# Batch 0 of a two-block kernel: loads in another order, identity products in waits, a new hand-written order, and stores by quarters

## The chip, the core and the metric

The kernel runs on one core of a Trainium2 chip. What is measured is the device time of one execution in microseconds; the profile adds the span of the core and the TensorE clock that the throttle granted. Before the change the time is 767.9 us (median of three runs, 767.73 to 767.93).

## The reference

```
# attention block: x (B,H,S,D) = (8,8,512,64), state (8,8,32,64)
scores  = scale * x @ state.T        # per batch and head, 512 x 32
xread   = softmax(scores,  -1) @ state
scores2 = scale * state @ x.T        # 32 x 512
sread   = softmax(scores2, -1) @ x
y = concat([xread, sread], axis=2)   # (B,H,544,64)
# bridge: (B,H,544,64) -> rows (B*544, 512)
# feed-forward block, w_in 512 x 2048, w_out 2048 x 512, both float64 inputs
h = rows @ w_in
g = where(h > 0, h, exp(min(h, 0)) - 1)      # elu
out = g @ w_out
```

## The kernel before

For each batch the 512 token rows go through attention and the feed-forward block. The attention of the tokens isn't multiplied out: `make_m` forms M = state · w_in, and `ffn1` multiplies the turned softmax `aT` straight by M (8 matmul records of 128x512 for two of its 16 blocks `fo`). `exp_part` on ScalarE and `max_part` on VectorE make the elu, `ffn2_row` multiplies by `w_out` into four PSUM banks, `o_ps` = banks 0 to 3. Batches 1 to 7 use two levels of a Strassen scheme for the second product; after batch 7, `states()` runs the 256 state rows of all batches at once, with one such level (`Strassen(1)`), and stores them.

The weights arrive as float64. Each of 32 pieces (512 KB of HBM) is made float32 by three ScalarE instructions (`convert_1`) and four VectorE instructions (`convert_2`), all within batch 0. Batch 0 is therefore unlike the others: TensorE, VectorE and ScalarE all have much to do, and their order is written out by hand.

That order is the string `plan` in `first_batch`. Each token is a step, put on its engine in this order, and every engine keeps it (`InOrder`). The names that matter here:

- `kT`, `kTc`: turn the states on TensorE, copy them out of PSUM on VectorE into the tile `kT`
- `x:b.i`, `xc:b.i`: turn half of x of batch b on TensorE, copy it out on ScalarE; `sc:b`: scores on TensorE into banks 6 and 7
- `mx`, `sd`, `tr`, `tm`, `su`, `tt` (batch.group, VectorE), `ps`, `pm` (GpSimd), `ae`, `te` (ScalarE): the two softmaxes; `tt` writes `aT`
- `sT`, `sTc`, `sr`, `src`: the state's own read (TensorE, ScalarE, TensorE, ScalarE)
- `w:k.1`, `w:k.2`: `convert_1` and `convert_2` of weight piece k; after `w:k.2` the next load is issued (`fetch`)
- `M:0.c.h`, `Mc:0.c.h`: a half of M and its copy; `F:fo` is `ffn1`, `R:fo` is `exp_part`, `E:fo` is `max_part`, `O:fo` is `ffn2_row`

`load_states` loads the states of all eight batches with eight transfers, four on the SP queue and four on the ACT queue; `load_x` loads one batch of x with four. The first code lines that run are

```
raw_states = load_states()
load_x(0, [sync, scalar])
for k in range(NRAW - 1):
    fetch()
```

The raw pieces, the raw states and turned x share one pool of `NRAW + 4` = 11 buffers (tag `w`). At the end of batch 0 the four banks `o_ps` are copied out, bank 0 first, bank 3 last; banks 1 and 3 on VectorE. `ffn1` of batch 1 writes banks 4, 5, 3, 4, ... in turn, so its third block needs bank 3 back. From batch 1 on VectorE, ScalarE and GpSimd are ordered by the scheduler of the language, which also draws the weight sums of batch 1 (tiles `t_w`, `t`, `w_out`) in between the last steps of batch 0 on VectorE.

`states()` ends with eight stores of one batch each, 64 KB, all on the SP queue and all after the last step of the second product.

Of the kernel before, what the change touches and what calls it, by code (L numbers as in the profile page):

```python
# [10 lines left out]
FP32 = mybir.dt.float32  # L11
# [14 lines left out]
def kernel(  # L26
# [15 lines left out]
    B, H, S, D = x.shape  # L42
    NS = state.shape[2]
    DM, DF = moe_w_in.shape
    P = 128
    R = S // P
    NP = H // 2
    G = 2
    FO = DF // P
    FC = DF // 512  # L50
    SB = S + NS
    NB = S // 32
    NRAW = 7
# [6 lines left out]
    out_b = out.rearrange("(b s) c -> b s c", b=B)  # L60
# [4 lines left out]
    def pool(name, bufs, **kw):  # L65
        return ctx.enter_context(tc.tile_pool(name=name, bufs=bufs, **kw))

    cpool = pool("const", 1)
# [4 lines left out]
    work = pool("work", NRAW + 4)  # L73
# [6 lines left out]
    def bank(i):  # L80
        return psum[:, i]

    def pair(i):

        return psum[:, i : i + 2]
# [3 lines left out]
    class InOrder:  # L89
# [10 lines left out]
    tensor, sync, vector, scalar, gpsimd = (  # L100
        InOrder(e) for e in (nc.tensor, nc.sync, nc.vector, nc.scalar, nc.gpsimd)
    )
    matmul = tensor.matmul

    def transpose(out, in_):


        for t in range(2):
            rows = slice(t * 64, (t + 1) * 64)
            tensor.transpose(out[:, t], in_[rows], ident[rows, rows], tile_position=(t * 64, 0))  # L110
# [4 lines left out]
    ident = cpool.tile([P, P], FP32, name="ident")  # L115
# [6 lines left out]
    kT = cpool.tile([P, B, P], FP32, name="kT")  # L122
# [3 lines left out]
    x_t, st, m_t = {}, {}, {}  # L126
# [6 lines left out]
                out=x_t[b][:, r].rearrange("p (h d) -> p h d", d=D), in_=x_v[:, r]  # L133
            )

    def load_states():
        raw = work.tile([P, B, G, D], FP32, tag="w", name="s_sb")
        s_v = state.rearrange("b (m c) n d -> m c n b d", c=G)
        for m in range(NP):
            for c in range(G):  # L140
                (sync, scalar)[c].dma_start(out=raw[m * NS : (m + 1) * NS, :, c], in_=s_v[m, c])
        return raw

    def turn_states(raw):
        ps = st["k_ps"] = pair(6).rearrange("p t (b q) -> p t b q", q=64)
        for b in range(B):
            transpose(ps[:, :, b], raw[:, b].rearrange("p c d -> p (c d)"))

    def load_weights(src):
        _, n, k = src.shape  # L150
        raw = work.tile([P, n, k], moe_w_in.dtype, tag="w", name="raw")
        sync.dma_start(out=raw, in_=src)
        return raw
# [39 lines left out]
    def load_w_in(c, k):  # L193

        h, n = divmod(k, 2)
        rows = slice(2 * n, 2 * n + 2)
        cols = slice(c * 512 + h * 256, c * 512 + (h + 1) * 256)
        return w_in[:, 2 * c + h, rows], load_weights(w_in_v[:, rows, cols])

    def load_w_out(fo):  # L200
        raw = load_weights(w_out_v[:, fo : fo + 1])
        return w_out[:, fo : fo + 1], raw
# [168 lines left out]
    def max_part(fo, e, ps):  # L371
        vector.scalar_tensor_tensor(
            out=g_all[:, fo, : ps.shape[-1]], in0=e, scalar=-1.0, in1=ps,
            op0=ALU.add, op1=ALU.max,
        )
# [255 lines left out]
    def first_batch():  # L631

        plan = """
            kT kTc x:0.0 xc:0.0 w:0.1 x:0.1 xc:0.1 w:0.2 w:1.1 sc:0 mx:0.1 w:2.1 tr:0.1 tr:0.0
            tm:0.1 w:3.1 tm:0.0 ps:0.1 mx:0.0 w:1.2 ps:0.0 ae:0.1 ae:0.0 te:0.1 sT:0 sd:0.0 sd:0.1  # L640
            te:0.0 su:0.1 sTc:0 su:0.0 pm:0.1 w:4.1 M:0.0.0 w:3.2 pm:0.0 Mc:0.0.0 w:7.1 sr:0 tt:0.1
            tt:0.0 w:4.2 F:0 src:0 w:8.1 w:2.2 F:1 R:0 w:5.1 E:0 M:0.0.1 w:8.2 Mc:0.0.1 R:1 F:2
            w:5.2 w:9.1 O:0 E:1 w:10.1 w:9.2 R:2 F:3 w:10.2 w:6.1 M:0.1.0 O:1 E:2 Mc:0.1.0 w:6.2 R:3
            w:12.1 E:3 F:4 w:7.2 w:11.1 O:2 w:12.2 w:13.1 R:4 w:11.2 M:0.1.1 F:5 w:14.1 w:13.2 O:3
            R:5 Mc:0.1.1 E:4 w:16.1 E:5 w:14.2 F:6 w:17.1 M:0.2.0 w:16.2 F:7 R:6 w:15.1 E:6 O:4
            w:17.2 Mc:0.2.0 w:18.1 w:15.2 F:8 R:7 w:18.2 O:5 w:21.1 E:7 R:8 w:21.2 M:0.2.1 w:19.1
            O:6 E:8 w:23.1 w:19.2 Mc:0.2.1 F:9 w:23.2 w:24.1 O:7 w:25.1 w:24.2 w:20.1 w:25.2 F:10
            R:9 O:8 w:20.2 w:22.1 E:9 R:10 w:22.2 M:0.3.0 w:26.1 F:11 E:10 O:9 Mc:0.3.0 w:26.2 R:11
            w:27.1 E:11 M:0.3.1 w:29.1 w:27.2 F:12 O:10 R:12 w:29.2 Mc:0.3.1 w:30.1 E:12 F:13 w:31.1
            w:30.2 O:11 R:13 w:31.2 w:28.1 E:13 x:1.0 w:28.2 F:14 xc:1.0 x:1.1 R:14 F:15 xc:1.1 E:14  # L650
            sc:1 R:15 O:12 mx:1.0 mx:1.1 ae:1.0 tr:1.0 ae:1.1 tr:1.1 tm:1.0 sT:1 tm:1.1 ps:1.0 O:13
            sd:1.0 sTc:1 sd:1.1 E:15 ps:1.1 te:1.0 su:1.0 te:1.1 pm:1.0 su:1.1 sr:1 pm:1.1 tt:1.0
            O:14 src:1 tt:1.1 M:1.0 O:15 Mc:1.0
        """.split()
        make_identity(nc, ident)
        o_ps = [bank(c) for c in range(R)]
        order = [lambda k=k: load_w_in(0, k) for k in range(4)]
        for c in range(1, FC + 1):
            if c < FC:
                order += [lambda c=c, k=k: load_w_in(c, k) for k in range(4)]  # L660
            order += [lambda fo=fo: load_w_out(fo) for fo in range(4 * c - 4, 4 * c)]
        w, h, e = [], {}, {}

        def fetch():
            if len(w) < len(order):
                w.append(order[len(w)]())
            elif 1 not in x_t:
                load_x(1, [sync])

        raw_states = load_states()  # L670
        load_x(0, [sync, scalar])
        for k in range(NRAW - 1):
            fetch()
        groups = {
            "mx": column_max, "tr": turn_scores, "ae": column_exp, "tm": row_max,
            "ps": row_subtract, "te": row_exp, "su": row_sum, "pm": row_scale,
            "tt": turn_tokens, "sd": column_total,
        }
        whole = {
            "sc": scores, "sT": turn_state, "sTc": copy_state, "sr": state_read,  # L680
            "src": keep_read,
        }
        for step in plan:
            name, _, num = step.partition(":")
            num = [int(i) for i in num.split(".") if i]
            if name == "kT":
                turn_states(raw_states)
            elif name == "kTc":
                vector.tensor_copy(out=kT.rearrange("p b (t q) -> p t b q", t=2), in_=st["k_ps"])
                fetch()  # L690
            elif name in groups:
                groups[name](*num)
            elif name in whole:
                whole[name](*num)
            elif name == "w":
                (convert_1, convert_2)[num[1] - 1](*w[num[0]])
                if num[1] == 2:
                    fetch()
            elif name == "F":
                h[num[0]] = ffn1(0, num[0])  # L700
            elif name == "R":
                e[num[0]] = exp_part(h[num[0]])
            elif name == "E":
                max_part(num[0], e[num[0]], h[num[0]])
            elif name == "O":
                ffn2_row(o_ps, num[0])
            elif name == "x":
                turn_x(*num)
            elif name == "M":
                make_m(*num)  # L710
                if len(num) == 2:
                    make_m(1, 1, first=4)
            elif name == "xc":
                copy_x(*num)
            else:
                assert name == "Mc", step
                if len(num) == 3:
                    copy_half(*num)
                else:
                    for g in range(G):  # L720
                        copy_m(*num, g, scalar.copy)
        for g in range(G):
            copy_m(1, 1, g, scalar.copy)
        for i in range(2):
            o_sb = opool.tile([P, 2, DM], FP32, name="o_sb")
            for c in range(2):
                (scalar.copy, vector.tensor_copy)[c](out=o_sb[:, c], in_=o_ps[2 * i + c])
            store(0, i, o_sb)

# [26 lines left out]
    def states():  # L756
        for i in second:
            i.restore()
        for fo in range(FO):
            ffn1_state(fo)  # L760
        half = Strassen(1)
        half.sums()
        for f in half.steps():
            f()
        for b in range(B):
            c, i = divmod(b, P // NS)
            sync.dma_start(
                out=out_b[b, S:SB], in_=half.o_sb[c][i * NS : (i + 1) * NS].rearrange("p n c -> p (n c)")
            )

    first_batch()
    load_x(2, [sync])
# [35 lines left out]
```

## Time and profile before

Busy time of the engines in some stretches of the span (us from its start; records of matmuls overlap, so a TensorE busy for the whole stretch may have room in it):

| stretch | TensorE | VectorE | ScalarE | granted clock | DMA GB/s |
|---|---|---|---|---|---|
| 0 to 5 | 0.34 | 0.00 | 0.00 | 1.00 | 125 |
| 5 to 10 | 1.93 | 1.22 | 1.28 | 1.00 | 247 |
| 10 to 15 | 1.91 | 0.09 | 2.98 | 1.00 | 386 |
| 25 to 30 | 2.75 | 4.72 | 4.94 | 0.99 | 108 |
| 60 to 80 | 20.00 | 19.28 | 19.65 | 1.00 | 200 |
| 80 to 100 | 20.00 | 18.74 | 16.87 | 1.00 | 79 |
| whole span, 766.1 | 735.7 | 416.2 | 311.0 | 0.994 | 46 |

Up to some 40 us no engine is busy all the time; from there to about 110 us three are; after that TensorE alone is. A waiting instruction is put down to what released it last. "Chain" below is the chain of work that ended last, followed back from the last instruction. A name like `ps<-aT,m_sb` is what an instruction writes and reads, with the tile names of the code; `issue` means that the profile shows nothing waited for.

### The profile page before, as it was taken

To read this page: it belongs to the slowest core of one execution; us is meant where nothing else is said; L and a number is where in the kernel's file an instruction comes from. 1 tells how busy PE (TensorE), PEld (TensorE's weight loads), DVE (VectorE), ACT (ScalarE), POOL (GpSimd) and SP (SyncE) were. 2 spreads that over 40 slices of the span, in tenths; PEclk is the share of its full clock that TensorE was granted. 3 is DMA by queue.
4 is the path that set the end of the run, shared out by engine and by line. 5 is a ranking of instruction groups with operands and counts; after the bars stand their busy time and mean duration, and the time that the engine had idled before them with its cause. 6 is when DMAs were issued, how large, how long until landed. Compare 5 with 4: busy or idle time off the path is not lost.

```text
span 766.1 us, 10566 instructions
## 1 busy us (share of the span) xinstructions
PE 735.7 (96%) x4352; PEld 502.0 (66%) x4352; DVE 416.2 (54%) x737; ACT 311.0 (41%) x557; POOL 35.1 (5%) x38
## 2 busy tenths in 40 slices
PE   3599999999999999999999999999999999999996
PEld 1234444368955787478946895578747894689885
DVE  2999989638246533655354824663365535534230
ACT  4799874553036312641065303631264106400420
POOL 0200002002000200010000200020001000000000
PEclk9899999999999999999999999999999999999999
DMA  9555400400210021002000021002100000000001
GB/s 282 216 196 212 110 1 1 110 1 10 46 56 1 1 56 56 0 2 56 28 27 1 13 44 55 1 1 56 56 1 2 1 31 25 0 1 28 29 1 27
DMA packets 44849, 35.29 MB, mean 46 GB/s; under 512 B 36352, under 2 KB 36352, under 8 KB 44800
## 3 DMA queue, kind: packets, MB, share of 16 engines
q1 hardware_dynamic: 41632, 33.82, 14.6%
q10 hardware_dynamic: 3168, 0.79, 0.5%
q8 instruction: 34, 0.56, 0.3%
q14 instruction: 15, 0.12, 0.1%
HBM read 25.69 MB, written 8.91 MB: 45 GB/s over the span
## 4 chain that ended last, share of the span: by engine, by line
PE 92%; DVE 5%; DMA 1%; ACT 1%; issue 0%; ACTq 0%; DVEq 0%
PE ps L95 92%; DVE t_w L95 1%; DMA x_sb<-in_x_dram 1%; DVE w_in L95 1%; DVE total_t L95 1%; DVE w_out L95 0%; DMA s_sb<-in_state_dram 0%; ACT raw L95 0%; DVE top L95 0%; DVE aT L95 0%; DVE top_t L95 0%; ACT xT L95 0%; DVE t_sb L95 0%; ACT a_s L95 0%; ACT e_sb L95 0%; DVE o_sb L95 0%
## 5 line engine op out<-in xcount | busy, mean ns | idle before, releaser
L95 PE MATMUL ps<-w_out,g_all 128*128 128x256 f32 (+2 forms) x1088 | 252.2, 385 | 0.0
L95 PE MATMUL ps<-aT,m_sb 128*128 128x512 f32 x512 | 228.4, 600 | 6.2 <-DVE aT L95 3.3
L95 PEld LDWEIGHTS ps<-w_out,g_all 128*128 128x128 f32 x1088 | 188.8, 190 | 57.4 <-issue 35.9
L95 PEld LDWEIGHTS ps<-aT,m_sb 128*128 128x128 f32 x512 | 96.3, 192 | 128.6 <-issue 118.6
L95 DVE SCALAR_TENSOR_TENSOR g_all<-e_sb,ps 128x512 f32<-128x512 f32 (+1 forms) x144 | 94.2, 656 | 118.5 <-ACT e_sb L95 118.5
L95 ACT ACTIVATE e_sb<-ps 128x512 f32<-128x512 f32 (+1 forms) x144 | 82.5, 573 | 179.0 <-PE ps L95 161.3
L95 DVE TENSOR_TENSOR o_sb<-o_sb,ps 128x128 f32<-128x128 f32 (+2 forms) x122 | 43.8, 359 | 138.5 <-PE ps L95 96.9
L95 PE MATMUL ps<-t_w,s 128*128 128x256 f32 x480 | 107.2, 379 | 0.0
L95 PEld LDWEIGHTS ps<-t_w,s 128*128 128x128 f32 x480 | 90.7, 190 | 12.1
L95 ACT ACTIVATE e_sb<-e_sb 128x512 f32<-128x512 f32 (+1 forms) x144 | 87.3, 606 | 4.5
L95 ACT COPY o_sb<-ps 128x512 f32<-128x512 f32 (+1 forms) x34 | 19.1, 562 | 165.2 <-PE ps L95 115.9
L95 ACT ACTIVATE raw<-raw 128x512 f32<-128x512 uint32 x64 | 43.6, 682 | 1.0
L95 POOL TENSOR_TENSOR t_sb<-t_sb,top_t 128x512 f32<-128x512 f32 x16 | 17.6, 1108 | 536.0 <-DVE top_t L95 536.0
L95 PE MATMUL ps<-w_in,kT 64*32 64x512 f32 (+1 forms) x576 | 33.5, 553 | 0.0
L95 DVE TENSOR_TENSOR g_all<-g_all,s 128x512 f32<-128x512 f32 (+1 forms) x30 | 27.8, 926 | 9.6 <-PE ps L95 9.6
L95 PE MATMUL ps<-t_w,g_all 128*128 128x128 f32 (+1 forms) x240 | 32.0, 282 | 0.0
L95 DVE TENSOR_REDUCE top<-ps 128x1 f32<-128x512 f32 x16 | 11.0, 685 | 38.6 <-PE ps L95 38.6
L95 PEld LDWEIGHTS ps<-t_w,g_all 128*128 128x128 f32 x240 | 30.3, 192 | 0.8
L95 DVE TENSOR_TENSOR s<-s,g_all 128x512 f32<-128x512 f32 (+1 forms) x30 | 27.0, 934 | 3.4 <-PE ps L95 3.4
L95 DVE TENSOR_TENSOR g_all<-g_all 128x512 f32<-128x512 f32 (+1 forms) x30 | 28.1, 937 | 0.6
L95 DVE TENSOR_TENSOR s<-g_all 128x512 f32<-128x512 f32 (+1 forms) x30 | 27.5, 937 | 0.6
L95 PE MATMUL ps<-xT_state,w_in 128*128 128x256 f32 x128 | 27.8, 379 | 0.0
(67 smaller groups left out, 476.4 us busy)
## 6 DMA issues: line engine op xcount, KB each, us to landing
raw<-in_moe_w_in_dram SPq DMA_DIRECT2D x16, 512.0 KB, 5.8
raw<-in_moe_w_out_dram SPq DMA_DIRECT2D x16, 512.0 KB, 3.7
out_dram<-o_sb SPq DMA_DIRECT2D x16, 512.0 KB, 2.6
x_sb<-in_x_dram SPq DMA_DIRECT2D x30, 256.0 KB, 4.4
x_sb<-in_x_dram ACTq DMA_DIRECT2D x2, 256.0 KB, 5.8
out_dram<-o_sb SPq DMA_DIRECT2D x8, 64.0 KB, 1.7
s_sb<-in_state_dram ACTq DMA_DIRECT2D x4, 64.0 KB, 3.1
s_sb<-in_state_dram SPq DMA_DIRECT2D x4, 64.0 KB, 2.8
```

The source lines that it names most:

```text
L95: ins = getattr(self.engine, name)(*args, **kw)
```

## The change

It touches batch 0 and the last stores:

1. x of batch 0 is loaded first; of the states only batch 0's, 32 KB on each of two queues, into a tile of its own (`s_first`). The states of batches 1 to 7 are loaded by eight transfers on SP once 12 weight pieces have been asked for, and turned by the new steps `kU` and `kUc` in mid-batch. Seven weight pieces instead of six are asked for ahead.
2. `Z:n` issues n products of the identity with itself into bank 3, which nobody reads. They are to keep TensorE active while it waits.
3. The order of batch 0 is another.
4. Bank 3 is copied out first at the end of batch 0, then 2, 1, 0.
5. `states()` stores a quarter of its result (128 rows by 256 columns) as soon as it is done; the last one is halved over the SP and ACT queues.

```diff
-    def load_states():
-        raw = work.tile([P, B, G, D], FP32, tag="w", name="s_sb")
...
+    state_v = state.rearrange("b (m c) n d -> c m n b d", c=G)
+
+    def load_states(b0, b1, engines=None):
+        shape = [P, b1 - b0, G, D]
+        if b0 == 0:
+            raw = cpool.tile(shape, FP32, name="s_first")
+        else:
+            raw = work.tile(shape, FP32, tag="w", name="s_sb")
+        for c in range(G):
+            if b0 == 0:
+                engines[c % len(engines)].dma_start(out=raw[:, 0, c], in_=state_v[c, :, :, 0])
+                continue
+            for m in range(NP):
+                sync.dma_start(
+                    out=raw[m * NS : (m + 1) * NS, :, c], in_=state_v[c, m, :, b0:b1]
+                )
         return raw
...
-            kT kTc x:0.0 xc:0.0 w:0.1 x:0.1 xc:0.1 w:0.2 w:1.1 sc:0 mx:0.1 w:2.1 tr:0.1 tr:0.0
-            tm:0.1 w:3.1 tm:0.0 ps:0.1 mx:0.0 w:1.2 ps:0.0 ae:0.1 ae:0.0 te:0.1 sT:0 sd:0.0 sd:0.1
...
+            kT kTc x:0.0 xc:0.0 x:0.1 w:0.1 xc:0.1 w:0.2 w:1.1 sc:0 Z:16 tr:0.0 tr:0.1 w:2.1 tm:0.0
+            tm:0.1 ps:0.0 w:3.1 mx:0.1 mx:0.0 ps:0.1 w:1.2 ae:0.0 te:0.1 ae:0.1 sd:0.0 su:0.1 w:5.1
+            M:0.0.0 sd:0.1 pm:0.1 w:3.2 Mc:0.0.0 te:0.0 sT:0 w:4.1 tt:0.1 su:0.0 sTc:0 w:5.2 pm:0.0
+            w:8.1 Z:8 sr:0 tt:0.0 src:0 w:2.2 Z:3 F:0 w:6.1 F:1 w:8.2 R:0 M:0.0.1 R:1 E:0 Mc:0.0.1
+            E:1 O:0 w:9.1 w:4.2 w:10.1 w:9.2 F:2 w:7.1 w:6.2 M:0.1.0 F:3 R:2 w:7.2 Mc:0.1.0 O:1
...
+            O:10 w:27.2 R:13 R:12 w:28.2 x:1.0 w:31.1 O:11 E:12 E:13 xc:1.0 w:31.2 x:1.1 O:12 xc:1.1
+            sc:1 O:13 mx:1.1 mx:1.0 ae:1.1 tr:1.0 ae:1.0 tr:1.1 sd:1.0 sT:1 tm:1.0 tm:1.1 ps:1.0
+            F:14 sTc:1 sd:1.1 ps:1.1 te:1.0 sr:1 R:14 su:1.0 F:15 te:1.1 pm:1.0 E:14 src:1 su:1.1
+            O:14 R:15 tt:1.0 pm:1.1 E:15 tt:1.1 M:1.0 O:15 Mc:1.0
...
         def fetch():
+            if len(w) == 12 and len(raw_states) == 1:
+                raw_states.append(load_states(1, B))
...
-        raw_states = load_states()
         load_x(0, [sync, scalar])
-        for k in range(NRAW - 1):
+        raw_states = [load_states(0, 1, [sync, scalar])]
+        for k in range(NRAW):
             fetch()
...
+            elif name == "Z":
+                for i in range(num[0]):
+                    matmul(bank(3)[:, :P], ident, ident, start=True, stop=True)
...
-        for i in range(2):
+        for i in (1, 0):
             o_sb = opool.tile([P, 2, DM], FP32, name="o_sb")
-            for c in range(2):
+            for c in (1, 0):
                 (scalar.copy, vector.tensor_copy)[c](out=o_sb[:, c], in_=o_ps[2 * i + c])
...
-        for f in half.steps():
+        for n, f in enumerate(half.steps()):
             f()
-        for b in range(B):
-            c, i = divmod(b, P // NS)
-            sync.dma_start(
-                out=out_b[b, S:SB], in_=half.o_sb[c][i * NS : (i + 1) * NS].rearrange("p n c -> p (n c)")
-            )
+            quarter = {1: (0, 0), 4: (1, 1), 5: (1, 0), 6: (0, 1)}.get(n)
+            if quarter is None:
+                continue
+            c, q = quarter
+            cols = slice(q * DM // 2, (q + 1) * DM // 2)
+            engines = [sync, scalar] if n == 6 else [sync]
+            k = P // len(engines)
+            for i, e in enumerate(engines):
+                b = (c * P + i * k) // NS
+                e.dma_start(
+                    out=out_b[b : b + k // NS, S:SB, cols], in_=half.o_sb[c][i * k : (i + 1) * k, 0, cols]
+                )
```

## The prediction, made before the changed kernel ran

> **What bounds the kernel now.** I read the chain of waits first (columns: start in us, length, what).
>
> ```profile
> 4.11 7.00 DMA x_sb<-in_x_dram
> ...
> 32.35 3.80 PE ps L95 x4
> ...
> 39.80 73.06 PE ps L95 x293
> 112.86 0.01 DVEq L95
> ...
> 136.09 623.87 PE ps L95 x3736
> 759.97 0.02 issue
> 759.99 0.37 ACT o_sb L95
> ```
>
> Four stretches. Up to 39.8 the end is set by the x load, which lands at 11.11, and by the work behind it; then TensorE alone carries the chain to 112.9; then VectorE to 136.09; then TensorE without a pause to the last copy at 760, and a tail to 766.1. Only time taken from the first, third and last stretch, or from TensorE's work, shortens the run. Next, busy times by stretch (TensorE, its weight loads, VectorE, ScalarE, GpSimd, clock, DMA share, GB/s):
>
> ```profile
> 14.91:32.30 17.39, 6.75 (x104) 3.14 (x104) 16.01 (x33) 16.27 (x31) 4.15 (x4) 0.93 0.64 239
> 30.00:35.00 5.00, 2.65 (x3) 1.18 (x4) 4.83 (x10) 1.94 (x4) 0.00 (x0) 0.50 0.55 192
> 41.00:60.00 19.00, 19.00 (x74) 7.85 (x73) 18.21 (x34) 17.80 (x30) 0.00 (x0) 1.00 0.61 206
> 112.90:131.30 18.40, 18.40 (x138) 8.25 (x137) 18.13 (x29) 7.77 (x17) 5.13 (x4) 1.00 0.00 1
> 131.30:136.05 4.75, 2.99 (x7) 1.13 (x6) 4.75 (x9) 2.45 (x4) 0.00 (x0) 1.00 0.19 79
> ```
>
> VectorE is full from 14.9 on (16.0 of 17.4, 18.2 of 19, 18.1 of 18.4), so whatever starts earlier on TensorE must be fed by a VectorE that starts earlier too. The clock is 0.50 in 30 to 35, where `F:0` and `F:1` run: weight loads every 0.86 us there, every 0.43 later. Third, TensorE's waits up to 136.1 (engine, writes <- waited for: total, times, longest):
>
> ```profile
> PE ps L95 <- DMA s_sb<-in_state_dram: 5.3, 2, 4.3
> PE ps L95 <- ACT a_s L95: 5.1, 1, 5.1
> PE ps L95 <- DVE aT L95: 3.3, 1, 3.3
> PE ps L95 <- DVE o_sb L95: 1.8, 1, 1.8
> ```
>
> The last is the only TensorE wait after 40 us: the third block of batch 1 wants bank 3, whose copy VectorE ends at 136.04. Last, single pieces (timeline; throughput of the first 13 us in 40 slices):
>
> ```profile
> 8.08 1.28 ACT L95 ACT_TABLE_LOAD   x1 [8.08 <-DMA x_sb<-in_x_dram]
> 22.01 1.58 DVE L95 TENSOR_SCALAR w_in<-w_in 128x512 f32<-128x512 f32 x2
> 40.32 0.88 DVE L95 TENSOR_SCALAR w_in<-w_in 128x512 f32<-128x512 f32 x2
> 760.38 3.63 SPq L95 DMA_DIRECT2D out_dram<-o_sb  x8
> GB/s 0 0 0 0 0 92 214 176 213 224 259 252 174 108 169 115 237 287 288 288 243 219 217 216 221 220 224 237 262 312 330 399 391 391 384 378 378 391 397 397
> ```
>
> Runs of 256 bytes (x, states) move at about 218 GB/s, runs of 2 KB (weights) at 390. Over 16 engines that is 19 and 84 ns a run and engine.
>
> **What the Trainium skill says.** (1) "TensorE: Matmul & The Clock Gate", Part 1: after about 3.4 us without activity the clock is halved, and about that much activity restores it. The trace has the half clock from 30 on, 1 us after the last of some sparse work, and the full one again from about 36.7 on, 4 us into `F:0`; but none after the 5.1 us without work before 22.96. The way back agrees, the threshold for falling doesn't. (2) "DMA: Bandwidth & Descriptors", Why a DMA increments its semaphore by 16: a transfer runs on the largest number of engines up to 16 that divides the slowest dimension of both sides. All transfers before have 32 or 128 there; nothing in the trace tests it. (3) "SBUF — State Buffer", Who interferes with whom: a VectorE tensor_scalar and GpSimd block each other. The trace agrees: the pair above takes 1.58 beside GpSimd, 0.88 alone.
>
> **Part by part, likeliest case.**
> Loads. x (1.05 MB) no longer stands behind 0.52 MB of states. Bytes flow from 1.65 as before; at 218 to 288 GB/s, 3.6 to 4.8 us, I take 4.6: until 6.3. The new state transfers have four heads as slowest dimension in HBM, so by (2) four engines carry both: 64 runs of 19 ns, 1.2, until 7.5. Spread over 16 they'd take 0.3. From last byte to landing 0.8 (the first states: issued 0.73, bytes until some 2.3, landed 3.13). So the states land at 8.3. Behind them `kT` 0.35 and its copy 0.25, 8.95 with waits; then, new on the path, the table load of 1.28, which waits for that copy as it did before and was hidden by the x load; `x:0.0` (0.95) runs beside it. ScalarE starts `xc:0.0` at 10.35, before at 11.99: **1.65 gained**.
> Order up to `F:0`. Before, `F:0` came 20.4 after `xc:0.0`. VectorE now does a fourth conversion (`w:5.2`) ahead of the last `tt`: +2.9 beside GpSimd. `w:1.2` no longer meets GpSimd (-0.7), nor does the second row sum (-0.4), and `mx` moves behind `tr` and `tm`, which saves a wait (-0.2). Sum +1.6: `F:0` at 32.35, as before.
> `Z` steps. 27 products of 128 columns by 2 records of 0.13 are 7.2 us, all in gaps: `Z:16` runs while VectorE does 6 us up to `w:1.2`, `Z:8` while ScalarE converts, `Z:3` before `tt:0.0` ends. Cost nothing on the path. They are worth 2.4: `F:0` and `F:1` in 3.45, not 5.85. But `O:0` then waits for `E:0`, behind two conversions (4.5) and itself 0.7: `O:0` at 37.6. The same work was done before at 39.8: **2.2 ahead**.
> The later states cost TensorE 14 transposes, 0.65, in a saturated stretch, and VectorE 1.1 (7/8 of the 1.22 copy). With 2.25 per conversion and 0.69 per `E` from `E:1` on, VectorE then makes `O:8` wait 0.55 for `w:24.2`. Of the 2.2, **1.0 is left** at `sc:1` (111.9). The SP queue's eight transfers wait for nothing that is soon needed.
> Third stretch. The built order of the new kernel has on VectorE, from `mx:1.1` to the bank 3 copy, one `E` and one sum `t` more (1.2), one bank copy less (0.6), and fewer sums beside GpSimd (1.1 of excess). So 22.6 for 23.1. Bank 3 is first of the copies, but stands behind all the sums of the second weights, where before some came after it: the reordering hardly helps. `O:15` isn't held up: `E:15` ends 14.9 after `sc:1`, TensorE gets there after 14.8. The third block starts at 134.6 for 136.09: **1.5**.
> Tail. Before: eight issues, the last at 763.56, landing 1.7 later, end 0.8 after. Three quarters now leave before the end, hidden by products of 3.5 us each. The last one leaves at 760.38 on two queues. By (2) each half has 2 batches as slowest dimension, so both lie on the same two engines: 64 runs of 1 KB each. A run is 46 ns by the line between 19 and 84: 2.95 instead of 0.17. End 760.38 + 1.7 - 0.17 + 2.95 + 0.8 = 765.7: **0.4**. Bounds: on 16 engines 763.1 (3.0 gained); at 84 ns a run 768.1 (2.0 lost).
> Sum 1.5 + 0.4 = 1.9: 766.0.
>
> **Rivals.**
> B, *all transfers use 16 engines*. For: everything before does, and the queues share them. Against: the rule in (2). States 0.9 earlier, head 2.4; tail 3.0; 762.5.
> C, *the clock falls anyway, or the states land late*. For: the clock fell before though transposes and reads ran until 29.0; 2.5 us without work remain ahead of `F:0`. Against: eleven of the last sixteen us now have TensorE work. `F:0` and `F:1` again take 5.85 and `O:0` comes 1.5 later: the head is lost, tail 0.4: 767.5.
> D, *slower*: the tail at 84 ns a run (-2.0) with the head lost as in C. For: HBM writes in short runs are unmeasured here, and VectorE has no slack. Against: both must come together. 769.9.
> A bank 3 wait as long as before is contained in A.
>
> **How the numbers follow.** A 0.46, B 0.26, C 0.16, D 0.12. The step "faster by over 0.2%" is 766.4; A, uncertain by about 1 us, is beyond it 7 times in 10 (0.32), B always (0.26), C hardly ever (0.04): faster 0.62. Same: 0.14 of A and 0.12 of C, 0.26. Slower: D, 0.12. The range goes from 761.8, a little under B, to 768.4, over C; D is left out.
>
> **What would show it.** First x copy on ScalarE at about 10.35, with the table load directly ahead. `F:0` near 32.35 with weight loads every 0.43. First `w_out` product at 37.6. Scores of batch 1 end near 111.9. One wait of TensorE for `o_sb`, under 1 us, near 134. The last two stores landing over 4 us after issue; under 2 would be B. I'd be wrong most simply if the early transfers land by 7.3, or if the clock is 0.5 after 30.

## The result and the profile after

The changed kernel takes 771.0 us (median of four runs, 770.5 to 771.7) against 767.8 for the kernel before on the same chip: a ratio of 1.0043, with a 95% interval of 1.0026 to 1.0061. I had predicted 766.0, faster, with a range up to 768.4. The span of the profiled run went from 766.1 to 768.7.

The chain of waits of the changed kernel, thinned to the lines that answer to those of before (start in us, length, what):

```profile
2.03 10.44 DMA s_first<-in_state_dram
...
13.34 1.28 ACT L95
...
14.63 1.07 ACT xT L95 x2
...
41.84 73.81 PE ps L95 x309
...
126.05 636.25 PE ps L95 x3792
762.32 0.37 ACT o_sb L95
```

The first line is the news. x no longer bounds the head: the ACT queue moved the last of it at 7.1 us, where before it landed at 11.1. In its place stands one transfer of 32 KB, half of batch 0's states, which took 10.44 us and landed at 12.47. The table load of 1.28 follows, and ScalarE starts the first x copy at 14.63; before it was 11.99. From there the kernel only carries this on. TensorE's stretch without a pause begins at 41.84 (before 39.80), and the last copy starts at 762.32 (before 759.99). The tail after it takes 6.4 us, before 6.1. So 2.3 + 0.3 = 2.6 of span.

TensorE's waits in the first 140 us of the changed kernel (total, times, longest):

```profile
PE ps L95 <- DMA s_first<-in_state_dram: 12.6, 1, 12.6
...
PE ps L95 <- DVE g_all L95: 2.1, 2, 1.3
...
PE ps L95 <- DVE aT L95: 1.3, 1, 1.3
```

The waits of before for x (2.3) and `a_s` (5.1, now filled with identity products and down to 0.9) are gone, and so is the 1.8 for `o_sb`. The state wait replaced the first. The last was replaced by a wait of 1.3 for `g_all`: the chain enters TensorE at 126.05 from `E:14`, ahead of `O:14`, not from a bank copy.

The same kernel by stretches (columns as before: TensorE, weight loads, VectorE, ScalarE, GpSimd, clock, DMA share, GB/s), from the first x copy to `F:0`:

```profile
14.63:36.77 22.14, 15.72 (x175) 12.27 (x175) 17.76 (x37) 20.97 (x39) 4.41 (x4) 0.92 0.54 181
```

`F:0` and `F:1` now have the full clock, as intended: 3.70 us for the two, before 5.85. The 0.92 of the row says that a half clock lies ahead of them, and the timeline of TensorE names the place (start, length, operation, number, and the idle time before it):

```profile
30.61 3.00 PE L95 MATMUL ps<-ident 128*128 128x128 f32 x16
...
36.77 3.70 PE L95 MATMUL ps<-aT,m_sb 128*128 128x512 f32 x8 [1.25 <-DVE aT L95]
```

Sixteen records are eight products. `Z:8` took 3.00 us here; eight such products take 1.95 where the clock is full (in the kernel with more of them, below). By the clock column the half clock lasted from about 29.4 to 32.8, so most of it fell on products that nobody needs, and the rest on `sT`.

### The profile page after: what moved, and what is told of

Read it like the earlier page. It is cut to its first block, busy times and chain, and to the rows that moved or that the text cites. A ratio compares the mean times of both kernels' runs of the same rounds, so it can differ in the third digit from the quotient of the medians.

```text
span 768.7 us, 10667 instructions
## 1 busy us (share of the span) xinstructions
PE 740.6 (96%) x4406; PEld 508.9 (66%) x4406; DVE 414.4 (54%) x738; ACT 311.2 (40%) x557; POOL 35.4 (5%) x38
## 4 chain that ended last, share of the span: by engine, by line
PE 93%; DVE 4%; DMA 1%; ACT 1%; issue 0%; ACTq 0%; DVEq 0%
PE ps L95 93%; DMA s_first<-in_state_dram 1%; DVE w_in L95 1%; DVE t_w L95 1%; DVE top L95 0%; DVE total_t L95 0%; DVE top_t L95 0%; DVE w_out L95 0%; ACT xT L95 0%; DVE t_sb L95 0%; ACT L95 0%; ACT raw L95 0%; DVE aT L95 0%; ACTq L95 0%; DVE g_all L95 0%
## 5 line engine op out<-in xcount | busy, mean ns | idle before, releaser
L95 PE MATMUL ps<-aT,m_sb 128*128 128x512 f32 x512 | 226.0, 595 | 1.3 <-DVE aT L95 1.3
```

What stands on the lines that cost most here:

```text
L95: ins = getattr(self.engine, name)(*args, **kw)
```

## Why the states land so late: one cause, four kernels

The two issues of `s_first` in the changed kernel, and what the DMA queues moved from 10 to 11 us (q1 is SP's, which carries the weights by then; q10 is ACT's, which has only the states left):

```profile
L95 SPq DMA_DIRECT2D s_first<-in_state_dram x1: 741/741/741, 1.9 to 1.9; - x1
L95 ACTq DMA_DIRECT2D s_first<-in_state_dram x1: 1922/1922/1922, 2.0 to 2.0; - x1
```

```profile
DMA packets 222, 0.37 MB, mean 369 GB/s; under 512 B 47, under 2 KB 47, under 8 KB 222
...
q1 hardware_dynamic: 181, 0.36, 100.6%
q10 hardware_dynamic: 41, 0.01, 4.8%
```

The issue on ACT takes 1.92 us by itself. The ACT queue is through with x at 7.1, moves nothing until 8.6, and then its 128 runs of 256 bytes leave at about 40 a microsecond until 11.85. In the stretch above they are 4.8% of the time of the 16 engines, while 181 packets, mostly weight runs of 2 KB, pass beside them. The profile shows no engine standing idle, so this looks like two queues taking turns on the same engines. On four engines the 128 runs are 32 each, and 40 a microsecond is one run every 100 ns and engine: about one weight run of 84 and one state run of 19. The 32 so take 3.3 us, where alone they would take 0.6. The 1.5 us in which the ACT queue moved nothing came on top; what caused them is open.

My theory after the result was this one, the **turns**, though I put it at two weight runs for each state run, which the rate does not bear out. Its first rival was **four engines**: that a transfer with so short a slowest dimension is slow by itself. Its second was that **the order and the clock**, not the landing, cost the time.

**Both halves on the SP queue**, ahead of the weights:

```diff
-        raw_states = [load_states(0, 1, [sync, scalar])]
+        raw_states = [load_states(0, 1, [sync])]
```

> The changed kernel with both transfers of batch 0's states on the SP queue, ahead of the weights on the same queue; still four engines. Theory 1 (the ACT queue's states shared four engines with weight runs of 2 KB from the SP queue and got one turn for every two of them): nothing is left to share with, 64 runs of 19 ns behind x, landing near 8, first x copy near 10.3 instead of 14.6, about 766.7 us. Theory 2 (a transfer on four engines with its long issue is slow by itself): landing still near 12, about 771.

Measured: 768.2 (12 runs, 766.9 to 768.7), 0.9999 of before with an interval of 0.9991 to 1.0008. The chain of this kernel:

```profile
2.65 6.07 DMA s_first<-in_state_dram
...
10.93 1.07 ACT xT L95 x2
```

Still four engines, the same bytes, the same order of batch 0. But on its own queue the transfer stands ahead of the weights, lands at 8.72 instead of 12.47, and the first x copy comes 3.70 earlier. The last copy starts at 758.63, 3.69 earlier: the head passes on whole. That speaks against both rivals. (I had predicted a landing at 8.3.) In the medians it is 2.9 and not 3.7, because most kernels with the 27 products run in two groups some 1.3 us apart; more of that below. The lower group, 766.85 to 767.15, is near the 766.7 expected.

**The states in four transfers of 32 rows**, two on each queue, x still first:

```diff
-                engines[c % len(engines)].dma_start(out=raw[:, 0, c], in_=state_v[c, :, :, 0])
+                engines[m % len(engines)].dma_start(
+                    out=raw[m * NS : (m + 1) * NS, 0],
+                    in_=state_v[:, m, :, 0].rearrange("c n d -> n c d"))
```

> The changed kernel with batch 0's states in four transfers of 32 rows, both heads of a pair together, two per queue: 8 runs per engine and queue on all sixteen engines, instead of 32 on four. (The weights then wait for the first landing of x, at about 5.) Theory 1: a quarter of the turns, landing near 7, about 766. Theory 2: the same, as nothing is on four engines. A third theory, that whatever stands behind x on the ACT queue lands late: still near 12 and 771.

Measured: 767.85 (766.5 to 768.1, 12 runs). The states landed at 8.47, later than the 7 expected, and the first x copy came at 10.77. Half of them are still on the ACT queue, but it doesn't starve: spread over sixteen engines, each has only 8 of its runs, and no pause came. So for the states it took the few engines and the other queue's weights together, and either cure gives the same 3 us. Neither this run nor the last separates the turns from the pause; both went together.

**The states ahead of x**, on two queues and four engines as in the change:

```diff
-        load_x(0, [sync, scalar])
         raw_states = [load_states(0, 1, [sync, scalar])]
+        load_x(0, [sync, scalar])
```

> The changed kernel with batch 0's states issued ahead of x, still four engines and two queues. Theory 1: nothing to share with at that time, states at about 3.5, x at about 6.3, the table load of ScalarE hidden again, first x copy near 7.5, 7 us earlier than in the changed kernel: 764. Theory 2: states land 10 us after issue, at about 11: 769.5. If VectorE or the arrival of weights limits batch 0 instead, less than 7 us arrives at the end though the first copy is at 7.5.

Measured: 768.6 (767.0 to 770.0, 20 runs), ratio 1.0009, interval 1.0003 to 1.0016. The states landed at about 3.8, 3.1 us after their issue, before any weight run: four engines are not slow. But now the x half on the ACT queue is the last to be issued, and starves instead:

```profile
2.66 8.17 DMA x_sb<-in_x_dram
...
11.71 1.07 ACT xT L95 x2
```

It landed at 10.83, although x spreads over sixteen engines. So what seems to count is how many short runs an engine still has to move for the ACT queue when the weights begin: 64 for each transfer of x, for the states 32 on four engines and 8 on sixteen. This may also account for part of a line of before that I had read as mere bytes ahead: the x load of 7.00 us there is on the ACT queue too, its weights on SP. That part was not tested alone.

## The tail

**Each quarter stored in transfers of 32 rows**, otherwise as changed:

```diff
-            for i, e in enumerate(engines):
-                b = (c * P + i * k) // NS
-                e.dma_start(out=out_b[b : b + k // NS, S:SB, cols], in_=half.o_sb[c][i * k : (i + 1) * k, 0, cols])
+            for i in range(P // NS):
+                engines[i % len(engines)].dma_start(
+                    out=out_b[c * P // NS + i, S:SB, cols], in_=half.o_sb[c][i * NS : (i + 1) * NS, 0, cols])
```

> The changed kernel with every quarter stored in four transfers of 32 rows (the last four over both queues), so that all sixteen engines are used. If two engines carrying 64 runs each are what makes the tail 6.4 us, it falls to about 3.5 (issue of two per queue, 1.7 to landing, 0.8): 768.2. If the long issue or the HBM writes are what costs, it stays at about 6: 771.

Measured: 768.7 (766.9 to 769.1, 20 runs), 2.3 below the changed kernel, ratio to before 1.0006 with an interval of 1.0 to 1.0013. From the last copy to the end it took 3.5 us for 6.4. The DMA of the last 9.4 us, in 40 slices (busy tenths of 16 engines, then GB/s), first of the changed kernel, then of this one:

```profile
DMA  0000022222220000000010111111111111000000
GB/s 0 0 0 0 0 44 26 87 92 96 96 96 22 0 0 0 0 0 0 13 17 17 44 35 44 22 17 39 44 52 44 52 48 48 22 0 0 0 0 0
```

```profile
DMA  0313141410000000404141400000004646000000
GB/s 0 92 48 100 39 105 35 105 35 0 0 0 0 0 0 17 122 17 122 26 114 26 114 0 0 0 0 0 0 0 105 170 109 170 4 0 0 0 0 0
```

In the changed kernel the quarter of four batches moves at about 95 GB/s and the last quarter, two transfers of two batches, at some 40 to 50, for some 3.6 us. In 32-row transfers the last quarter is through in about 1 us. A busy share of 2 tenths and of 1 tenth and twice the rate for twice the batches are what the Trainium skill has in "DMA: Bandwidth & Descriptors", Why a DMA increments its semaphore by 16: four engines of 16 for four batches, two for two. At 48 GB/s over two, a run of 1 KB takes 43 ns, where I had taken 46.

**The kernel before with the stores of the change alone**:

> The kernel before with only the last stores of the change: four quarters as each is done, three of them as one transfer of 4 batches, the last as two of 2 batches. Theory 1 (the last two transfers run on two engines and take as long as the eight stores did): tail from the last copy to the end 6.1 to 6.5, so 767.8 to 768.3, no gain. Rival (in the changed kernel the tail was long for another reason, and early quarters help): tail 3.4, 765.0, as with 32-row transfers. In either case the first x copy stays at about 12 and F:0 at half clock.

Measured: 768.2 (767.6 to 768.4, 12 runs), ratio 1.0004, interval 0.9996 to 1.0013. The tail took 6.6 us (last copy at 759.21, end at 765.8). Three quarters leave early and save nothing, since the last one takes as long on two engines as all eight stores did on sixteen.

**The kernel before with the quarters in 32-row transfers**:

> The kernel before with nothing changed but the last stores: quarters as soon as done, each in transfers of 32 rows. The tail falls from 6.1 to about 3.2, everything ahead of it is as before: 764.9. If the early stores disturb the last products, less gain: 766 to 767.

Measured: 765.0 (764.5 to 765.5, 5 runs), ratio 0.9959, interval 0.9945 to 0.9973: tail 3.4 us. The idea of part 5 is worth 2.7 us of tail, and 3.2 in the medians of that chip (768.2 before); the shape of its transfers took that away.

## What the other parts are worth with the transfers mended

With states in 32-row transfers on ACT ahead of everything, all of x on SP and the weights behind it, and the tail in 32-row transfers, no short run has weight runs of the other queue beside it (the last of the states leaves at 5.5, the first weight run at 6.8). I call this base **split**.

```diff
-        load_x(0, [sync, scalar])
-        raw_states = [load_states(0, 1, [sync, scalar])]
+        raw_states = [load_states(0, 1, [scalar])]
+        load_x(0, [sync])
... (states and stores in 32-row transfers, as in the two runs above)
```

> The changed kernel with the three causes of delay at the edges mended: batch 0's states in four transfers of 32 rows, first and alone on the ACT queue; x on the SP queue only, so that the weights stand behind it there and nothing of batch 0 shares an engine with them; quarters stored in transfers of 32 rows. Theory 1 (turns shared with weight runs): states at about 4, x at about 7, first x copy near 8 instead of 14.6, and 2.9 from the tail: about 761.4, between 760.7 and 762.5 by where the clock falls. If VectorE's conversions or the arrival of weights set the pace of batch 0, the copy is at 8 but the end gains only part: 763 to 765. If x on one queue is too slow to issue (four times 0.5 us), the copy is near 10: 763.

Measured (split_queues): 762.6 (761.9 to 763.5, 4 runs), ratio 0.9932, interval 0.9917 to 0.9947. The first x copy came at 8.83, `F:0` at 30.99, `O:0` at 36.07. The four times lie in two pairs, 761.9 and 763.4.

**Without the 27 products**:

```diff
-... sc:0 Z:16 tr:0.0 ...  w:8.1 Z:8 sr:0 ...  w:2.2 Z:3 F:0 ...
+... sc:0 tr:0.0 ...  w:8.1 sr:0 ...  w:2.2 F:0 ...
```

> The kernel split_queues without the 27 identity products. If they keep the clock up (my prediction gave them 2.4 at the first two blocks of F, of which some is lost behind VectorE): the clock falls ahead of F:0 in every run, as it did before, about 1.3 us more than the faster runs of split_queues, 762.0, with a narrow spread. If they are worth nothing, the same times and the same spread as split_queues.

Measured: 763.7 (763.3 to 764.1, 4 runs), 1.1 above split by the medians, with ranges that overlap and two pairs again (763.3 and 764.0), not the narrow spread expected. Its TensorE timeline:

```profile
20.05 2.45 PE L95 MATMUL ps<-w_in,kT 64*32 64x256 f32 x16 [5.13 <-ACT a_s L95]
...
31.19 5.18 PE L95 MATMUL ps<-aT,m_sb 128*128 128x512 f32 x8 [2.88 <-DVE aT L95]
```

The wait of 5.13 for `a_s` is the one of before. `M` after it took 2.45, where split takes 1.45 for the same 16 records (0.62 and 0.83), the state's read 1.93 for 1.10, and `F:0` with `F:1` 5.18 for 3.70: 3.3 us of TensorE. The last copy came at 757.83 for 756.55, so 1.3 later, 0.2 of which is the later first x copy (9.04). More than half of the lost TensorE time lay beside VectorE's work.

**With more products**, to close the last two gaps:

```diff
-            M:0.0.0 sd:0.1 ...  Z:3 F:0
+            M:0.0.0 Z:5 sd:0.1 ...  Z:8 F:0
```

> The kernel split_queues with five more identity products after the first half of M and eight instead of three ahead of F:0, so that the two waits of 1.5 and 2.8 us are filled. If what makes two groups of times is whether the clock falls in the wait ahead of F:0 or earlier: only the faster group is left, about 760.7, weight loads of F:0 every 0.43. If the fall follows from something else (the waiting for the states, say), two groups as before; if the products hold up TensorE, about 0.5 slower.

Measured: 762.1 (761.9 to 762.2, 4 runs), ratio 0.9924, interval 0.991 to 0.9939. There is one narrow group of times now and no record under full clock between 26 and 38 us. It is as fast as split's lower pair and not 760.7, as expected: a half clock that falls on products nobody needs seems to cost nothing. I take the two groups of the other kernels to be runs in which the clock fell before `F:0` and runs in which it fell in it. The six profiles of kernels with the 27 products agree: the changed kernel, both halves on SP, 32-row states and split, each profiled in a run of its lower group, have 3.70 for `F:0` and `F:1`; the states ahead of x and the 32-row tail, profiled at 768.9 and 769.1, have 5.40, after a wait of 2.8 for `aT`. That more products leave one group supports it; that every other time belongs to one of the two is inferred, as only one run of each kernel has a profile.

**The same with the banks copied out in the old order**, 0 to 3:

> split_more_z (states in four 32-row transfers on the ACT queue, x on SP, stores in 32-row transfers, Z:5 after M:0.0.0 and Z:8 before F:0) with one thing undone: at the end of batch 0 the banks are copied out in the old order, 0, 1, 2, 3. On VectorE this puts bank 1's copy ahead of two of the weight sums and bank 3's copy one sum earlier but one copy later. Theory 1 (the order of the copies is worth nothing, since the sums of the weights set the time of bank 3's copy): 762.1 as split_more_z, within 0.3, and bank 3's copy ends within 0.2 of where it did. Rival (bank 3 first is what took the 1.8 us wait for o_sb away): a wait of TensorE for o_sb of 1 to 1.8 comes back, 763.1 to 763.9.

Measured: 761.9 (761.8 to 761.9, 4 runs). Copies to `o_sb` on VectorE in this kernel, and in the one with bank 3 first:

```profile
131.49 0.69 DVE L95 COPY o_sb<-ps 128x512 f32<-128x512 f32 x1
```

```profile
131.77 1.28 DVE L95 COPY o_sb<-ps 128x512 f32<-128x512 f32 x2
```

Bank 3 is the copy above, 1.8 us behind bank 1's, and the first of the pair below: it starts at 131.49 and at 131.77, and this kernel's `O:14` is 0.27 ahead to begin with. No wait for `o_sb` came back. Part 4 is worth nothing that shows: the sums decide when the copy comes, not its place among the copies.

**The old order of batch 0 on split**, with only `kU` and `kUc` put in, without products, and then with 37 of them in its gaps:

```diff
             ... R:7 w:18.2 kU O:5 w:21.1 E:7 R:8 kUc w:21.2 ...   (both)
+            ... sc:0 Z:16 ...  M:0.0.0 Z:5 ...  w:7.1 Z:8 sr:0 ...  Z:8 F:0 ...   (the second)
```

> split_queues (states in four 32-row transfers on the ACT queue, x on SP, stores in 32-row transfers, bank 3 first) with the order of batch 0 taken from the kernel before: no Z steps, only kU put in after w:18.2 and kUc after R:8. Theory 1 (loads and stores carry the gain, the order itself is worth about a microsecond): before_tail32 ran 765.0 with the first x copy at 12.2; here it comes at about 8.8, F:0 20.4 later at half clock, the states of batches 1 to 7 cost TensorE 0.65, so 765.0 - 3.4 + 0.65 = 762.3, at most 0.5 from split_no_z's 763.66 less 1.3. Rival 1 (the new order is worth 1.5 or more): 763.8 to 765. Rival 2 (the old order is the better one once the loads are mended): under 761.5.

> split_old_order with identity products in the gaps of the old order: Z:16 after sc:0, Z:5 after M:0.0.0, Z:8 before sr:0, Z:8 before F:0. Separates the products from the order. Theory 1 (with the old order VectorE feeds TensorE no earlier, so the full clock in F:0 and F:1 saves the 2.4 us there but most of it is lost to E:0 and the conversions ahead of O:0): 0.5 to 1.5 under split_old_order, 761 to 762. Rival 1 (old order plus products does all that the new order does): equal to split_more_z, 762.1, or below. Rival 2 (the products get in the way of M or of the reads and delay them): equal to or above split_old_order.

Measured: 763.1 (762.9 to 763.7) and 762.1 (762.0 to 762.4), four runs each. The first lies between the 762.3 expected and the rival's 763.8. The second equals the new order with as many products (medians 762.09 both); the first is 0.6 below the new order without products (the ranges overlap). These pairs ran on two chips, on which the kernel before took 767.8 (old order) and 768.2 (new); as ratios to it they are 0.9929 and 0.9924, and 0.9943 and 0.9945, with intervals of about 0.0015 to each side. The waits of TensorE in the old order with products:

```profile
PE ps L95 <- DVE o_sb L95: 1.8, 1, 1.8
```

Its 1.8 for bank 3 stands as before, although bank 3 is copied first here. So it is the new order that takes this wait away; it pays for it ahead of `F:0` (22.1 us after the first x copy, 20.4 in the old one) and with the 1.3 for `g_all`. In sum the new order is worth nothing that these runs can tell. 37 products are worth 1.0 us in the old order and 1.6 in the new one. Two pieces of part 1 have no run of their own: the seventh weight piece asked for ahead, and the later loading of the other states.

## Why the prediction was wrong, step by step

- **States land at 8.3: the step that failed.** They landed at 12.47. I had the right engines (four, by the skill's rule) and about the right time for a run, but added the runs up as if x, states and weights went one after the other in the order of their issue: "four engines carry both: 64 runs of 19 ns, 1.2, until 7.5". The weights, issued on the other queue while the first bytes moved, were left out. Measured, the ACT queue was through with x at 7.1 for 6.3, stood still until 8.6, then took 3.3 us for its 32 runs an engine where 1.2 had stood for all 64, and the landing came 0.6 after the last. The turns would account for the 3.3; why the queue stood still is open. The long ACT issue was not foreseen either. With both halves on SP and the four engines kept, the landing is 8.72 and the time that of before; the whole loss against before goes with this one term. Rival C named late states, but sized its loss by the clock alone.
- **Table load on the path, 1.28 ahead of the first x copy:** right, to the hundredth. The copy came 4.28 later than predicted; 4.17 of it is the landing.
- **`F:0` 22.0 after that copy, `O:0` 5.25 after `F:0`:** measured 22.1 and 5.07. Right, and so was the full clock in `F:0`. That no half clock was left was wrong: it is 0.5 from 29.4 to 32.8, on `Z:8` and the turns before it. The "2.4" is near what `F:0` and `F:1` gained (5.85 to 3.70), but only part of it reaches the end, since TensorE then waits 0.8 for `g_all` of `E:0`, as the same part said; 27 products were worth 1.1 by the medians, 37 of them 1.0 to 1.6. The reading that before the clock had not fallen after the wait of 5.1 was wrong as well: it was at half already (last section).
- **`O:0` to the scores of batch 1, 73.7 + 0.55:** measured 73.86. The wait of `O:8` didn't come. The later states cost the old order 0.8 here (73.83 for 73.06), 0.65 predicted.
- **Third stretch 0.5 shorter:** right in size (646.6 from there to the last copy, before 647.1), for another reason. I expected the bank wait to remain, under 1 us; it went, and one of 1.3 at `O:14` came.
- **Tail 0.4 shorter:** 0.3 longer. Engines and run time were right (46 ns predicted, 43 measured). By the throughput row the last quarter begins at 13 to 17 GB/s, so that its bytes took 3.6 us for 2.95, and some 1.3 passed from the last of them to the end, where I had taken 0.8; 0.5 of this came back, as they began 1.0 after the issue and not 1.5.

The sum: 4.3 in the head, 0.7 in the tail, 0.5 given back between them, 4.5 in all. The predicted 766.0 stood for a span of 764.2; it was 768.7.

## What to carry to other kernels

When a small transfer is moved, ask what the other queue sends on the same engines until it lands: here a load of 32 short runs an engine was priced by the long runs that passed between, not by its bytes. Put what the path waits for first, in a shape that spreads over all engines, on a queue with nothing behind it on the other that can get in between. And test each part of a bundle with the others mended: here two good parts (early states and x, early stores) were hidden by the shape of their transfers, the products gave a microsecond, and the new order and the banks nothing that these runs can tell.

## What the runs showed of the hardware

- The same load of 32 KB landed 3.1 us after its issue when first in its queue, 6.1 behind x on the SP queue, and 10.4 behind x on the ACT queue beside weight runs of the other; an x load of 256 KB took 8.2 in that place.
- Issues don't cost the same: 0.74 us on SP and 1.92 on ACT for the two halves of the states behind x, 1.44 on ACT for the same half ahead of it, 0.45 to 0.60 for each of the 32-row transfers first on ACT.
- The clock column isn't proof: it reads 1.00 too where the profile holds no clock record yet, and in the kernel before its first record is at 26.5 us. The length of known products tells. The scores and the eight turns of `a_s` in that kernel, first in batch 0, then in batch 1:

```profile
15.89 1.96 PE L95 MATMUL ps<-xT,kT 64*32 64x512 f32 x16 [1.65 <-ACT xT L95]
22.96 1.97 PE L95 MATMUL ps<-ident,a_s 128*128 128x128 f32 x8 [5.12 <-ACT a_s L95]
...
111.66 1.09 PE L95 MATMUL ps<-xT,kT 64*32 64x512 f32 x16
116.22 1.04 PE L95 MATMUL ps<-ident,a_s 128*128 128x128 f32 x8
```

So the 1.00 in the first rows of the table before was not full speed, and nothing here shows a clock that outlasted 5.1 us without work. The scores of batch 0 take 1.96 in all fourteen profiles. What the products do first is to bring the full clock earlier: on split its first record is at 16.2 to 17.5 us with them, at 23.3 and 34.2 without.

- "TensorE: Matmul & The Clock Gate", Part 1, of the Trainium skill has activity of about 3.4 us restore the clock. The spells at half clock here agree with that (3.4 us in the changed kernel, 6.8 before). When it falls goes by how busy TensorE was over 3.4 us, not by its longest wait: the waits in the 10 us before the fall in the changed kernel are all under 1.5. That kernel, then the one with the 32-row tail (TensorE's busy time is the second number, the clock the third from the end):

```profile
25.97:29.39 3.42, 1.39 (x19) 0.60 (x18) 3.20 (x11) 3.39 (x8) 0.95 (x1) 1.00 0.41 140
29.39:32.80 3.41, 3.41 (x19) 3.41 (x18) 3.31 (x6) 3.38 (x7) 0.35 (x1) 0.50 0.11 32
```

```profile
27.94:31.36 3.42, 2.01 (x18) 2.01 (x19) 3.20 (x9) 3.39 (x7) 1.30 (x1) 1.00 0.48 158
34.77:38.19 3.42, 1.18 (x3) 0.68 (x4) 3.28 (x7) 1.96 (x4) 0.00 (x0) 1.00 0.70 147
38.19:41.60 3.41, 3.41 (x5) 1.35 (x4) 3.27 (x7) 1.23 (x2) 0.00 (x0) 0.50 0.90 303
```

The first copy of x comes 0.25 apart in these two, but the ends of their 3.4 us stretches lie elsewhere, so the same pause ahead of the turns of `a_s` drops the clock in one and not in the other. In all fourteen profiles the eight falls in batch 0 follow stretches with 1.1 to 1.4 us busy, and no stretch with 1.95 or more was followed by one. That the two groups of times come from where these stretches happen to end is inferred.
